# Joint image and text attention block: batch 0's image V first, batch 1's x loaded between V rows, text scores, gate and text V in one run of 32-column tiles

## The chip, the cores and the metric

The kernel runs on one core of a Trainium2 chip. The metric is the device time of one execution in microseconds. TensorE (PE) multiplies, VectorE (DVE), ScalarE (ACT) and GpSimd (POOL) work on tiles in SBUF and PSUM, and the queues of SyncE (SP), ACT and POOL issue the transfers (DMA).

## The reference

Two batches, 256 image tokens and 32 text tokens each, width D = 1152, bfloat16. With `c` the conditioning vector of a batch:

```
mod_i = (silu(c) @ wmod_img).reshape(B, 6, 1, D)      # rows 0, 1, 2: shift, scale, gate
mod_t = (silu(c) @ wmod_txt).reshape(B, 6, 1, D)
hi = layernorm(x_img) * (1 + sci) + shi ;  ht = layernorm(x_txt) * (1 + sct) + sht
qi, ki, vi = split(hi @ wqkv_img) ;        qt, kt, vt = split(ht @ wqkv_txt)
q, k, v = concat([qt, qi]), concat([kt, ki]), concat([vt, vi])      # 288 tokens
a = softmax(q k^T * D**-0.5) v
out_i = x_img + gai * (a[:, 32:] @ wo_img) ;  out_t = x_txt + gat * (a[:, :32] @ wo_txt)
```

## The kernel before, in words

D is nine slabs of 128 (`KT` = 9, `K8` = 8). Weight blocks of 1152 x 1152 come in one after the other on SP's queue, into five slots that are used again: image scale (`w_sc_i`), image V (`w_v_i`, in pieces of one, one, one, two, two and two slabs), image shift, image Q, and so on to the text output weights. The two batches of image x come first of all, one transfer each.

Image rows are four tiles of 128 (`NIT` = 4; tiles 0 and 1 are batch 0, tiles 2 and 3 batch 1). Each tile is normed: for tiles 0 and 2 ACT makes the sums (`ln_sums`), for 1 and 3 DVE the statistics (`ln_stats`); DVE norms all four (`ln_norm`). PE transposes the normed rows, three slabs of one batch at a time (`x_transposes`), into PSUM tiles `tp`; ACT or DVE copies these to `xT_i` (line 250).

The scale row of the modulation is made on PE with `silu(c)` as the stationary operand in four tiles of 32 columns (`sc_rows`, into `sc_ps`); DVE turns it into columns (`sc_cols`, line 257) and multiplies `xT_i` with it into `hS_i` (`x_scale`, line 264). V is made from `hS_i`, without the shift, which is added to attention's result later. `v_open` accumulates V over the slabs; six accumulators of 512 columns stand open at once: two for each of the tiles 0 and 1 (`A0`), one for each of the tiles 2 and 3 (`A1`). The two remaining ones follow, and `v_last` makes the last 128 columns of all four tiles. `evac` copies an accumulator to `v_i`, on DVE and ACT in turns. Between these parts stand the shift row (`mod_rows_of`, PSUM tile `gps`) and V's own shift (`shift_v_rows`).

Then come Q and K of the image (`qk_img`, 162 matmuls of 512 columns), with the text branch worked in between on DVE and ACT, then Q and K of the text.

The attention part: scores of image tiles (`scores_img`, nine matmuls for a tile), text scores in tiles of 32 columns (`scores_txt`), softmax in three steps (`soft_max` the row maximum on DVE, `soft_exp` the exponential on ACT, `soft_div` the division on DVE with 32 columns copied on POOL), transposes of the probabilities (`p_transposes`, PSUM tile `pT_ps`, ACT copies to `pT`), text V (`v_txt`, two halves `r`, in tiles of 64 columns that hold both batches' 32 tokens), the image gate (`mod_rows`: a row in four tiles of 32 columns, copied by ACT, written to DRAM by POOL's queue, and read back to all partitions as `gb` by `img_gate_spread`), `attn_pair` for weights times V, and the output projections `out_img` and `out_txt`.

PSUM has two pools: `ps_mm` with six places and `ps_tr` with two. A new tile waits until the one that had its place has been read. `pin` (`tc.keep_in_program_order`) keeps an instruction in the order of the program on its engine; all matmuls and transposes are pinned.

All matmuls are recorded at line 61 (`mm`) and all transposes at line 64 (`tr`), so the tile names tell them apart: `sc_ps`, `tp`, `vps` (V), `gps` (modulation rows), `ps` (Q, K, text V, output), `sps` (scores), `pT_ps`, `aps` (attention).

Of the kernel before, what the change touches and what calls it, by code (L numbers as in the profile page):

```python
# [14 lines left out]
def kernel(  # L15
# [14 lines left out]
    nc = tc.nc  # L30
# [32 lines left out]
    def tr(*a, **k):  # L63
        return pin(nc.tensor.transpose(*a, **k))  # L64
# [37 lines left out]
    sc_v, v_v = wview(wmod_img, D), wview(wqkv_img, 2 * D)  # L102
    for b in range(B):
        nc.sync.dma_start(x_i[:, b * TPB:(b + 1) * TPB, :], x_img[b].rearrange("(p t) d -> p t d", t=TPB))  # L104

# [3 lines left out]
    for r0, r1 in ((0, 1), (1, 2), (2, 3), (3, 5), (5, 7), (7, KT)):  # L109
        nc.sync.dma_start(w_v_i[:, r0:r1, :], v_v[:, r0:r1, :])  # L110
    w_sh_i = load_w(2, wmod_img, 0)
    w_q_i = load_rows(3, wqkv_img, 0)
    w_sh_t = load_rows(0, wmod_txt, 0, (0, 1, 3, 6))
# [99 lines left out]

    xn_i = act.tile([P, NIT, D], bf, tag="A")
    hS_i = act.tile([P, KT, B * NI], bf, tag="Bt")
# [11 lines left out]

    sc_ps = ps_mm.tile([P, KT, LW], f32, tag="mm")

# [10 lines left out]
    def x_transposes(k0, b):  # L240
        tr_pool = b == 1 or k0 < 6
        tp = (ps_tr if tr_pool else ps_mm).tile([P, 3, NI], bf, tag="tr" if tr_pool else "mm", name="tp")
        for kt in range(k0, k0 + 3):
            for t in range(TPB):
                i = b * TPB + t
                tr(tp[:, kt - k0, t * P:(t + 1) * P], xn_i[:, i, kt * P:(kt + 1) * P], ident[:])
# [19 lines left out]

    VW = 512
    v_i = act.tile([P, NIT, D], bf, tag="A")
    accs = {}

    def v_open(ids, k0, k1, kt_major=True):
        for key in ids:
            if key not in accs:
                accs[key] = ps_mm.tile([P, VW], f32, tag="mm", name="vps")
        loop = [(kt, key) for kt in range(k0, k1) for key in ids] if kt_major else \
            [(kt, key) for key in ids for kt in range(k0, k1)]
        for kt, (i, cc) in loop:
            mm(accs[(i, cc)][:], lhsT=hS_i[:, kt, i * P:(i + 1) * P], rhs=w_v_i[:, kt, cc * VW:(cc + 1) * VW],
               start=(kt == 0), stop=(kt == KT - 1), skip_group_check=True)
            if kt == KT - 1:  # L280
                evac(v_i[:, i, cc * VW:(cc + 1) * VW], accs[(i, cc)][:])

    A0 = [(0, 0), (0, 1), (1, 0), (1, 1)]
    A1 = [(2, 0), (3, 0)]

    def ln_norm_dve(i, mv):
        ln_norm(x_i[:, i, :], mv[:, 0:1], ln_rstd(mv[:, 1:2], P), P, xn_i[:, i, :])

    def ln_norm_act(i, sm):
        ln_norm(x_i[:, i, :], sm[:, 0:1], ln_rstd(sm[:, 2:3], P, sign=-1.0), P, xn_i[:, i, :])  # L290

    s0 = ln_sums(x_i[:, 0, :], xn_i[:, 0, :])
    m1 = ln_stats(x_i[:, 1, :], P, between=silu_cols)
    ln_var(s0)
    ln_norm_dve(1, m1)
    ln_norm_act(0, s0)
    s2 = ln_sums(x_i[:, 2, :], xn_i[:, 2, :])
    m3 = ln_stats(x_i[:, 3, :], P)
    ln_var(s2)
    r3, r2 = ln_rstd(m3[:, 1:2], P), ln_rstd(s2[:, 2:3], P, sign=-1.0)  # L300
    ln_norm(x_i[:, 3, :], m3[:, 0:1], r3, P, xn_i[:, 3, :])
    ln_norm(x_i[:, 2, :], s2[:, 0:1], r2, P, xn_i[:, 2, :])
    for out in [x_transposes(k0, 0) for k0 in (0, 3, 6)]:
        out()
    sc_rows(0, 4)
    warm_up(3)
    sc_rows(4, 7)
    out01 = x_transposes(0, 1)
    out31 = x_transposes(3, 1)
    sc_rows(7, K8)  # L310
    sc_rows(K8, KT)
    out61 = x_transposes(6, 1)
    out01()
    sc_cols(0, 1)
    x_scale(0, 1, 0, step=1)
    sc_cols(1, 5)
    x_scale(1, 3, 0)
    v_open(A0, 0, 3)
    out31()
    out61()  # L320
    x_scale(0, 3, 1)
    sc_cols(5, KT)
    for k0 in (3, 6):
        for b in range(B):
            x_scale(k0, k0 + 3, b)
    v_open(A1, 0, 3)
    v_open(A0 + A1, 3, KT - 2)
    v_open(A0 + A1, KT - 2, KT, kt_major=False)

# [7 lines left out]

    v_open([(2, 1)], 0, KT)
    p_sh = mod_rows_of(w_sh_i, sT32)
# [3 lines left out]
    for kt in range(KT):  # L343
        for b in range(B):
# [4 lines left out]
            else:  # L349
                nc.scalar.activation(h, h, ACT.Identity, bias=sh_i[:, kt, b:b + 1], scale=sc1_i[:, kt, b:b + 1])  # L350
    v_open([(3, 1)], 0, KT)

    def v_last():
        vps = ps_mm.tile([P, NIT, P], f32, tag="mm")
        for i in range(NIT):
            for kt in range(KT):
                mm(vps[:, i, :], lhsT=hS_i[:, kt, i * P:(i + 1) * P], rhs=w_v_i[:, kt, 2 * VW:D],
                   start=(kt == 0), stop=(kt == KT - 1))
        evac(v_i[:, :, 2 * VW:D], vps[:])

# [129 lines left out]
    def v_txt(r):  # L490
        ps = ps_mm.tile([P, VC], f32, tag="mm")
        for kt in range(KT):
            for g in range(2):
                c0 = g * HD + r * VC
                mm(ps[64 * g:64 * g + NTT, :], lhsT=hT_t[:, kt, :], rhs=w_v_t[:, kt, c0:c0 + VC],
                   start=(kt == 0), stop=(kt == KT - 1), tile_position=(0, 64 * g))
        return ps
# [10 lines left out]

    def mod_rows(w_blk, si):
        gps = ps_mm.tile([P, VC], f32, tag="mm")  # L510
        for kt in range(KT):
            for g in range(NGG):
                mm(gps[32 * g:32 * g + 32, :], lhsT=sT32[:, kt, :], rhs=w_blk[:, kt, g * VC:(g + 1) * VC],
                   start=(kt == 0), stop=(kt == KT - 1), tile_position=(0, 32 * g))
        g_sb = work.tile([P, VC], bf, tag="garow")
# [8 lines left out]
    def img_gate():  # L524
        mod_rows(w_ga_i, 0)

# [7 lines left out]
    def txt_gate():  # L534
        mod_rows(w_ga_t, 1)
        for g in range(2):
            for b in range(B):
                r0 = 64 * g + 32 * b
                nc.gpsimd.dma_start(gbf[r0:r0 + NT, :, :],
                                    gsc[1, b, :].rearrange("(r g j) -> g r j", r=2, g=2)[g].partition_broadcast(NT))  # L540

    v_last()
    shift_v_rows()
# [58 lines left out]

    def p_transposes(b):
        pT = work.tile([P, 3, NTOK], bf, tag="pT")
        tiles = [(range(3), ps_tr)] if b == 0 else [((2,), ps_mm), (range(2), ps_tr)]
        for kjs, pool in tiles:
            pT_ps = pool.tile([P, 8 * P], bf, tag="tr" if pool is ps_tr else "mm", name="pT_ps")
            txt = [(2, pbs["t"], ident2 if b else ident)]
            img = [(qi, pbs[(b, qi)], ident) for qi in range(TPB)]
            for n, kj in enumerate(kjs):  # L610
                for qi, pb, perm in (txt + img if b else img + txt):
                    o = n * NTOK + qpos[b][qi]
                    k0 = kj * P - (NT * b if kj == 2 else 0)
                    tr(pT_ps[:, o:o + P], pb[:, k0:k0 + P], perm[:])
            pin(nc.scalar.copy(pT[:, kjs[0]:kjs[-1] + 1, :],
                               pT_ps[:, 0:len(kjs) * NTOK].rearrange("p (k n) -> p k n", n=NTOK)))
        pTs[b] = pT

    def attn_keys(tiles, first):
        for b, dt in tiles:  # L620
            for kj in range(2):
                mm(tiles[(b, dt)][:], lhsT=v_i[:, b * TPB + kj, dt * P:(dt + 1) * P], rhs=pTs[b][:, kj, :],
                   start=(first and kj == 0), stop=(not first and kj == 1))
# [24 lines left out]

    sp = {key: scores_img(*key) for key in I[:2]}
    soft_max(I[0], sp[I[0]], P)  # L650
# [3 lines left out]
    soft_exp(I[1])  # L654
    st = scores_txt()
    half = work.tile([NTT, NTOK], f32, tag="half", bufs=1)
    pin(nc.scalar.copy(half[:], st[NTT:P, :]))
    soft_div(I[1])
    img_gate()
    pin(nc.vector.tensor_add(half[:], st[0:NTT, :], half[:]))  # L660
    soft_max("t", half, NTT)
    soft_exp("t")
    for key in I[2:]:
        sp[key] = scores_img(*key)
    soft_max(I[2], sp[I[2]], P)
# [86 lines left out]
```

## Time and profile before

| | us |
|---|---|
| median of 6 runs | 118.44 |
| lowest and highest | 117.76, 118.86 |
| the profiled execution | 118.42 |
| its span in the profile | 116.3 |

| engine | busy us | share of the span |
|---|---|---|
| PE (matmul) | 110.5 | 95% |
| DVE | 72.0 | 62% |
| PE (weight load) | 63.4 | 55% |
| ACT | 44.8 | 39% |
| POOL | 12.3 | 11% |

The profile is of one execution; its span runs from the first instruction of the program to the last, and some 2 us of the execution lie around it. "Chain" is the work that ended last, followed back step by step to what released it. An issue line names the transfer, its size and the time from issue to landing.

### The profile page before, as it was taken

The numbers are of one execution on the slowest core, as the hardware profiler recorded it, in microseconds if no ns is written. First come the engines' busy times: TensorE is split into PE (matmuls) and PEld (weight loads), VectorE is DVE, ScalarE is ACT, GpSimd is POOL, SyncE is SP. The second block draws the span as 40 slices with busy tenths as digits, with TensorE's granted clock in tenths as the row PEclk, the third lists the DMA queues.
The fourth block names the chain that finished last, engine by engine and source line by source line (L and its number), as shares of the span: only waits on it lengthen the run. The fifth ranks groups of instructions, "written<-read, shape, count | busy, mean of one in ns | idle before, by whom it ended". The sixth has DMA issues, their size and how long they took to land.

```text
span 116.3 us, 2500 instructions
## 1 busy us (share of the span) xinstructions
PE 110.5 (95%) x1036; PEld 63.4 (55%) x1036; DVE 72.0 (62%) x151; ACT 44.8 (39%) x93; POOL 12.3 (11%) x34
## 2 busy tenths in 40 slices
PE   5988899999999999999999999999999999999990
PEld 2335544445574444445454457777866555666670
DVE  3578494063869999999996040017748666356571
ACT  5699620042652298825241233245747400100000
POOL 7300000000000000000000000004618000443000
PEclk9999999999999999999999999999999999999999
DMA  3999999999999999999999999999999999722223
GB/s 103 386 384 408 406 407 410 414 410 412 409 401 411 332 409 413 403 414 411 409 358 411 414 410 418 399 419 399 411 401 412 422 385 403 280 110 56 101 51 102
DMA packets 18917, 41.02 MB, mean 353 GB/s; under 512 B 1323, under 2 KB 1851, under 8 KB 18907
## 3 DMA queue, kind: packets, MB, share of 16 engines
q1 hardware_dynamic: 18032, 39.85, 88.8%
q0 software_dynamic: 480, 0.89, 2.3%
q10 hardware_dynamic: 395, 0.12, 0.4%
q8 instruction: 8, 0.13, 0.4%
q14 instruction: 2, 0.02, 0.0%
HBM read 39.52 MB, written 1.34 MB: 351 GB/s over the span
## 4 chain that ended last, share of the span: by engine, by line
PE 85%; DMA 8%; DVE 2%; SPq 1%; ACT 1%; issue 0%
PE ps L61 52%; PE vps L61 15%; DMA t<-in_wmod_img_dram 8%; PE gps L61 5%; PE aps L61 5%; PE sps L61 5%; DVE tmp L693 1%; PE pT_ps L64 1%; PE tp L64 1%; DVE o L694 1%; SPq L104 1%; ACT xT_i L250 1%; PE sc_ps L61 0%; SPq L108 0%; PE tpt L64 0%
## 5 line engine op out<-in xcount | busy, mean ns | idle before, releaser
L61 PE MATMUL ps<-xT_i,t 128*128 128x512 bf16 x162 | 35.7, 379 | 0.0
L61 PEld LDWEIGHTS <-t 128*128 128x128 bf16 x324 | 20.5, 98 | 19.1 <-issue 0.6
L435 DVE SCALAR_TENSOR_TENSOR acc_sh<-t,sTf,acc_sh 128x1152 f32<-128x1152 bf16 x16 | 21.4, 1408 | 0.0
L61 PE MATMUL ps<-t,aT 128*128 128x384 bf16 (+3 forms) x153 | 20.3, 308 | 0.0
L61 PE MATMUL vps<-t,hS_i 128*128 128x512 bf16 (+1 forms) x108 | 17.9, 326 | 0.0
L61 PEld LDWEIGHTS <-aT 128*128 128x128 bf16 (+1 forms) x153 | 13.0, 101 | 7.1 <-issue 0.8
L61 PEld LDWEIGHTS <-hS_i 128*128 128x128 bf16 x108 | 9.0, 98 | 8.7 <-DVE hS_i L264 0.4
L365 ACT CAST qkT<-ps 128x512 bf16<-128x512 f32 (+2 forms) x11 | 6.1, 552 | 15.0 <-PE ps L61 13.7
L693 DVE TENSOR_TENSOR tmp<-ps,gb 128x384 bf16<-128x384 f32 (+2 forms) x13 | 6.8, 526 | 7.9 <-PE ps L61 7.9
L580 POOL TENSOR_SCALAR pb<-e,rs 128x32 bf16<-128x32 f32 (+1 forms) x5 | 2.1, 416 | 74.7 <-DVE rs L577 74.6
L363 ACT ACTIVATE qkT<-ps 128x512 bf16<-128x512 f32 (+2 forms) x11 | 6.1, 561 | 8.7 <-PE ps L61 7.0
L61 PE MATMUL wps<-warm 128*128 128x512 bf16 x25 | 7.6, 460 | 1.5 <-DVE unit L127 1.5
L180 DVE CAST v_i<-vps 128x512 bf16<-128x512 f32 x5 | 3.5, 692 | 7.5 <-PE vps L61 7.5
L565 DVE TENSOR_REDUCE nmx<-sps 128x1 f32<-128x288 f32 x4 | 1.8, 458 | 9.9 <-PE sps L61 9.9
L61 PEld LDWEIGHTS <-sT 128*32 128x32 bf16 x180 | 4.7, 96 | 2.9 <-issue 2.3
L182 ACT CAST v_i<-vps 128x512 bf16<-128x512 f32 x4 | 2.3, 580 | 9.9 <-PE vps L61 9.9
L629 DVE TENSOR_SCALAR aT<-aps,svc 128x288 bf16<-128x288 f32 x9 | 4.3, 518 | 2.1 <-PE aps L61 2.1
L61 PE MATMUL sps<-qkT 128*128 128x288 bf16 (+1 forms) x54 | 5.5, 287 | 0.0
L61 PE MATMUL ps<-hT_t,t 128*128 128x64 bf16 x162 | 5.2, 193 | 0.0
L61 PE MATMUL gps<-t,sT 128*32 128x288 bf16 x144 | 5.2, 287 | 0.0
L61 PEld LDWEIGHTS <-warm 128*128 128x128 bf16 x25 | 2.5, 111 | 4.9 <-issue 1.9
L61 PE MATMUL aps<-pT,v_i 128*128 128x288 bf16 x36 | 5.1, 287 | 0.0
(110 smaller groups left out, 105.1 us busy)
## 6 DMA issues: line engine op xcount, KB each, us to landing
t<-in_wqkv_txt_dram SPq DMA_DIRECT2D x3, 2592.0 KB, 18.5
t<-in_wmod_img_dram SPq DMA_DIRECT2D x2, 2592.0 KB, 14.0
t<-in_wmod_txt_dram SPq DMA_DIRECT2D x2, 2592.0 KB, 18.7
t<-in_wqkv_img_dram SPq DMA_DIRECT2D x3, 864.0 KB, 13.8
t<-in_wqkv_img_dram SPq DMA_DIRECT2D x1, 2592.0 KB
t<-in_wo_img_dram SPq DMA_DIRECT2D x3, 864.0 KB, 9.2
t<-in_wqkv_img_dram SPq DMA_DIRECT2D x3, 576.0 KB, 10.0
t<-in_wmod_txt_dram SPq DMA_DIRECT2D x2, 864.0 KB, 12.8
```

The lines of the kernel that those rows point to most:

```text
L61: return pin(nc.tensor.matmul(*a, **k))
L64: return pin(nc.tensor.transpose(*a, **k))
L104: nc.sync.dma_start(x_i[:, b * TPB:(b + 1) * TPB, :], x_img[b].rearrange("(p t) d -> p t d", t=TPB))
L180: nc.vector.tensor_copy(out_ap, in_ap)
L182: nc.scalar.copy(out_ap, in_ap)
L363: nc.scalar.mul(out_ap, in_ap, SCALE)
L365: nc.scalar.copy(out_ap, in_ap)
L435: pin(nc.vector.scalar_tensor_tensor(acc, w_sh_t[:, kt, :], col, acc, op0=ALU.mult, op1=ALU.add))
L565: pin(nc.vector.reduce_max(nmx[0:qn, :], sps[0:qn, :], axis=AX.X, negate=True))
L580: pin(nc.gpsimd.tensor_scalar(pb[0:qn, NI + 2 * NT:NI + 3 * NT], e[0:qn, NI:NTOK], rs[0:qn, :], 0.0, op0=ALU.mult, op1=ALU.add))
L629: nc.vector.tensor_scalar(dst, tiles[(b, dt)][:], bias, None, op0=ALU.add)
L693: nc.vector.tensor_mul(tmp[:, 0:n], ps[:, 0:n], gb[:, b, c0:c0 + n])
```

## The change

At the start, only batch 0's x is loaded ahead of the scale weights. The two tiles of batch 1 come as two transfers of 288 KB, one behind V's second piece and one behind V's fourth. `w_q_i` is loaded in two pieces instead of three. The normed rows and V are kept in one tile for each batch (`xn_b`, `v_b`).

Batch 0 is normed, transposed and scaled in all nine slabs before batch 1's norms begin. V has accumulators of 384 columns: batch 0's six run over slabs 0 to 7; then come 12 transposes of batch 1, slab 8 for four accumulators, the other 6 transposes, slab 8 for the last two; batch 1's accumulators follow, two together and then one by one. `v_last` is gone. The evacuations of batch 0's V are assigned to ACT or DVE by a string. The PSUM places of `sc_ps` and of batch 0's `tp` change pools, and two warm-up matmuls stand between the scale rows instead of three.

In the attention part PE makes the scores of all four image tiles, then text scores, the image gate's rows and text V in one run. Text V is made in tiles of 32 columns, one for each half of the columns and each batch. The softmax steps follow in a new order; the gate row's copy and writes (`gate_row`) stand behind the division of the text rows. The probabilities of batch 0 are transposed in two parts (slabs 0 and 1, and slab 2), and slab 2's copies of both batches are made by DVE instead of ACT.

```diff
-    for b in range(B):
-        nc.sync.dma_start(x_i[:, b * TPB:(b + 1) * TPB, :], x_img[b].rearrange("(p t) d -> p t d", t=TPB))
+    nc.sync.dma_start(x_i[:, 0:TPB, :], x_img[0].rearrange("(p t) d -> p t d", t=TPB))
...
     for r0, r1 in ((0, 1), (1, 2), (2, 3), (3, 5), (5, 7), (7, KT)):
         nc.sync.dma_start(w_v_i[:, r0:r1, :], v_v[:, r0:r1, :])
+        if r0 in (1, 3):
+            i = TPB + r0 // 2
+            nc.sync.dma_start(x_i[:, i, :], x_img[1].rearrange("(p t) d -> t p d", t=TPB)[i - TPB])
     w_sh_i = load_w(2, wmod_img, 0)
-    w_q_i = load_rows(3, wqkv_img, 0)
+    w_q_i = load_rows(3, wqkv_img, 0, (0, 5))
...
-    sc_ps = ps_mm.tile([P, KT, LW], f32, tag="mm")
+    sc_ps = ps_tr.tile([P, KT, LW], f32, tag="tr")
...
-        tr_pool = b == 1 or k0 < 6
-        tp = (ps_tr if tr_pool else ps_mm).tile([P, 3, NI], bf, tag="tr" if tr_pool else "mm", name="tp")
+        tp = (ps_tr if b else ps_mm).tile([P, 3, NI], bf, tag="tr" if b else "mm", name="tp")
...
+    V0, V1 = [[(i, cc) for i in range(b * TPB, (b + 1) * TPB) for cc in range(NCH)] for b in range(B)]
...
-    s2 = ln_sums(x_i[:, 2, :], xn_i[:, 2, :])
-    m3 = ln_stats(x_i[:, 3, :], P)
-    ln_var(s2)
-    r3, r2 = ln_rstd(m3[:, 1:2], P), ln_rstd(s2[:, 2:3], P, sign=-1.0)
-    ln_norm(x_i[:, 3, :], m3[:, 0:1], r3, P, xn_i[:, 3, :])
-    ln_norm(x_i[:, 2, :], s2[:, 0:1], r2, P, xn_i[:, 2, :])
     for out in [x_transposes(k0, 0) for k0 in (0, 3, 6)]:
         out()
     sc_rows(0, 4)
-    warm_up(3)
     sc_rows(4, 7)
-    out01 = x_transposes(0, 1)
-    out31 = x_transposes(3, 1)
+    warm_up(1)
     sc_rows(7, K8)
+    warm_up(1)
     sc_rows(K8, KT)
-    out61 = x_transposes(6, 1)
-    out01()
     sc_cols(0, 1)
     x_scale(0, 1, 0, step=1)
     sc_cols(1, 5)
-    x_scale(1, 3, 0)
-    v_open(A0, 0, 3)
+    x_scale(1, 4, 0)
+    sc_cols(5, KT)
+    x_scale(4, KT, 0)
+    s2 = ln_sums(x_i[:, 2, :], xn_b[1][:, 0, :])
+    ln_var(s2)
+    m3 = ln_stats(x_i[:, 3, :], P)
+    r2, r3 = ln_rstd(s2[:, 2:3], P, sign=-1.0), ln_rstd(m3[:, 1:2], P)
+    ln_norm(x_i[:, 2, :], s2[:, 0:1], r2, P, xn_b[1][:, 0, :])
+    ln_norm(x_i[:, 3, :], m3[:, 0:1], r3, P, xn_b[1][:, 1, :])
+    v_open(V0, 0, K8)
+    out01, out31 = x_transposes(0, 1), x_transposes(3, 1)
+    out01()
     out31()
-    out61()
-    x_scale(0, 3, 1)
-    sc_cols(5, KT)
-    for k0 in (3, 6):
-        for b in range(B):
-            x_scale(k0, k0 + 3, b)
-    v_open(A1, 0, 3)
-    v_open(A0 + A1, 3, KT - 2)
-    v_open(A0 + A1, KT - 2, KT, kt_major=False)
+    x_scale(0, 6, 1)
+    v_open(V0[0:4], K8, KT, engines="AAVV")
+    x_transposes(6, 1)()
+    v_open(V0[4:], K8, KT, engines="AA")
+    x_scale(6, KT, 1)
+    v_open(V1[0:2], 0, KT)
...
-    v_open([(2, 1)], 0, KT)
+    v_open(V1[2:3], 0, KT)
...
-    v_open([(3, 1)], 0, KT)
...
+    for key in V1[3:]:
+        v_open([key], 0, KT)
...
-                c0 = g * HD + r * VC
-                mm(ps[64 * g:64 * g + NTT, :], lhsT=hT_t[:, kt, :], rhs=w_v_t[:, kt, c0:c0 + VC],
-                   start=(kt == 0), stop=(kt == KT - 1), tile_position=(0, 64 * g))
+                for b in range(B):
+                    c0, r0 = g * HD + r * VC, 64 * g + NT * b
+                    mm(ps[r0:r0 + NT, :], lhsT=hT_t[:, kt, NT * b:NT * b + NT], rhs=w_v_t[:, kt, c0:c0 + VC],
+                       start=(kt == 0), stop=(kt == KT - 1), tile_position=(0, r0))
...
-    v_last()
     shift_v_rows()
...
-    sp = {key: scores_img(*key) for key in I[:2]}
+    sp = {key: scores_img(*key) for key in I}
+    st = scores_txt()
+    img_gate()
+    vt = [v_txt(0)]
+    half = work.tile([NTT, NTOK], f32, tag="half", bufs=1)
     soft_max(I[0], sp[I[0]], P)
     soft_exp(I[0])
     soft_max(I[1], sp[I[1]], P)
     soft_div(I[0])
     soft_exp(I[1])
-    st = scores_txt()
-    half = work.tile([NTT, NTOK], f32, tag="half", bufs=1)
+    soft_max(I[2], sp[I[2]], P)
+    soft_div(I[1])
+    soft_exp(I[2])
+    soft_max(I[3], sp[I[3]], P)
+    soft_div(I[2])
     pin(nc.scalar.copy(half[:], st[NTT:P, :]))
-    soft_div(I[1])
-    img_gate()
+    soft_exp(I[3])
     pin(nc.vector.tensor_add(half[:], st[0:NTT, :], half[:]))
     soft_max("t", half, NTT)
+    soft_div(I[3])
     soft_exp("t")
-    for key in I[2:]:
-        sp[key] = scores_img(*key)
-    soft_max(I[2], sp[I[2]], P)
-    soft_exp(I[2])
     soft_div("t")
-    soft_max(I[3], sp[I[3]], P)
-    soft_exp(I[3])
-    soft_div(I[2])
-    soft_div(I[3])
-    p_transposes(0)
-    for r in range(2):
-        v_txt_out(r, v_txt(r))
-    p_transposes(1)
+    gate_row()
+    v_txt_out(0, vt[0])
+    vt.append(v_txt(1))
+    p_transposes(0, (0, 1), ps_tr, nc.scalar.copy)
+    v_txt_out(1, vt[1])
+    p_transposes(0, (2,), ps_mm, nc.vector.tensor_copy)
+    p_transposes(1, (2,), ps_mm, nc.vector.tensor_copy)
+    p_transposes(1, (0, 1), ps_tr, nc.scalar.copy)
     img_gate_spread()
```

More of the change, by code (lines that the diff above doesn't have):

```diff
@@ L212, in ln_norm @@
         pin(nc.vector.tensor_scalar(out_ap, x_ap, mean, rstd[0:np_, :], op0=ALU.subtract, op1=ALU.mult))
-    xn_i = act.tile([P, NIT, D], bf, tag="A")
+    xn_b = [act.tile([P, TPB, D], bf, tag="A%d" % b, name="xn%d" % b) for b in range(B)]
     hS_i = act.tile([P, KT, B * NI], bf, tag="Bt")
@@ L240, in x_transposes @@
     def x_transposes(k0, b):
-        tr_pool = b == 1 or k0 < 6
-        tp = (ps_tr if tr_pool else ps_mm).tile([P, 3, NI], bf, tag="tr" if tr_pool else "mm", name="tp")
+        tp = (ps_tr if b else ps_mm).tile([P, 3, NI], bf, tag="tr" if b else "mm", name="tp")
         for kt in range(k0, k0 + 3):
             for t in range(TPB):
-                i = b * TPB + t
-                tr(tp[:, kt - k0, t * P:(t + 1) * P], xn_i[:, i, kt * P:(kt + 1) * P], ident[:])
+                tr(tp[:, kt - k0, t * P:(t + 1) * P], xn_b[b][:, t, kt * P:(kt + 1) * P], ident[:])
         dst = xT_i[:, k0:k0 + 3, b * NI:(b + 1) * NI]
@@ L265, in x_scale, with v_open @@
                                             op0=ALU.mult))
-    VW = 512
-    v_i = act.tile([P, NIT, D], bf, tag="A")
+    v_b = [act.tile([P, TPB, D], bf, tag="A%d" % b, name="v%d" % b) for b in range(B)]
     accs = {}
-    def v_open(ids, k0, k1, kt_major=True):
+    def v_open(ids, k0, k1, engines=None):
         for key in ids:
             if key not in accs:
[L274 to L278, printed above, removed]
+                accs[key] = ps_mm.tile([P, CH], f32, tag="mm", name="vps")
+        for kt, (i, cc) in [(kt, key) for kt in range(k0, k1) for key in ids]:
+            mm(accs[(i, cc)][:], lhsT=hS_i[:, kt, i * P:(i + 1) * P], rhs=w_v_i[:, kt, cc * CH:(cc + 1) * CH],
                start=(kt == 0), stop=(kt == KT - 1), skip_group_check=True)
             if kt == KT - 1:
-                evac(v_i[:, i, cc * VW:(cc + 1) * VW], accs[(i, cc)][:])
-    A0 = [(0, 0), (0, 1), (1, 0), (1, 1)]
-    A1 = [(2, 0), (3, 0)]
+                dst = v_b[i // TPB][:, i % TPB, cc * CH:(cc + 1) * CH]
+                if engines:
+                    pin((nc.scalar.copy if engines[ids.index((i, cc))] == "A" else nc.vector.tensor_copy)(
+                        dst, accs[(i, cc)][:]))
+                else:
+                    evac(dst, accs[(i, cc)][:])
+    V0, V1 = [[(i, cc) for i in range(b * TPB, (b + 1) * TPB) for cc in range(NCH)] for b in range(B)]
     def ln_norm_dve(i, mv):
-        ln_norm(x_i[:, i, :], mv[:, 0:1], ln_rstd(mv[:, 1:2], P), P, xn_i[:, i, :])
+        ln_norm(x_i[:, i, :], mv[:, 0:1], ln_rstd(mv[:, 1:2], P), P, xn_b[i // TPB][:, i % TPB, :])
     def ln_norm_act(i, sm):
-        ln_norm(x_i[:, i, :], sm[:, 0:1], ln_rstd(sm[:, 2:3], P, sign=-1.0), P, xn_i[:, i, :])
-    s0 = ln_sums(x_i[:, 0, :], xn_i[:, 0, :])
+        ln_norm(x_i[:, i, :], sm[:, 0:1], ln_rstd(sm[:, 2:3], P, sign=-1.0), P, xn_b[i // TPB][:, i % TPB, :])
+    s0 = ln_sums(x_i[:, 0, :], xn_b[0][:, 0, :])
     m1 = ln_stats(x_i[:, 1, :], P, between=silu_cols)
@@ L350 @@
                 nc.scalar.activation(h, h, ACT.Identity, bias=sh_i[:, kt, b:b + 1], scale=sc1_i[:, kt, b:b + 1])
-    v_open([(3, 1)], 0, KT)
[L353 to L359, printed above, removed]
+    for key in V1[3:]:
+        v_open([key], 0, KT)
     def qk_evac(out_ap, in_ap, blk):
@@ L507, in v_txt_cols, with mod_rows @@
         return r0, v_t[r0:r0 + NT, c0:c0 + P]
-    def mod_rows(w_blk, si):
+    def mod_rows(w_blk):
         gps = ps_mm.tile([P, VC], f32, tag="mm")
@@ L514, in mod_rows, with mod_row_out @@
                    start=(kt == 0), stop=(kt == KT - 1), tile_position=(0, 32 * g))
+        return gps
+    def mod_row_out(gps, si):
         g_sb = work.tile([P, VC], bf, tag="garow")
@@ L524, in img_gate, with gate_row @@
     def img_gate():
-        mod_rows(w_ga_i, 0)
+        rows["gi"] = mod_rows(w_ga_i)
+    def gate_row():
+        mod_row_out(rows["gi"], 0)
     def img_gate_spread():
@@ L534, in txt_gate @@
     def txt_gate():
-        mod_rows(w_ga_t, 1)
+        mod_row_out(mod_rows(w_ga_t), 1)
         for g in range(2):
@@ L601, with p_transposes @@
     pTs = {}
[L603 to L617, printed above, removed]
+    def p_transposes(b, kjs, pool, copy):
+        pT_ps = pool.tile([P, 8 * P], bf, tag="tr" if pool is ps_tr else "mm", name="pT_ps")
+        txt = [(2, pbs["t"], ident2 if b else ident)]
+        img = [(qi, pbs[(b, qi)], ident) for qi in range(TPB)]
+        for n, kj in enumerate(kjs):
+            for qi, pb, perm in (txt + img if b else img + txt):
+                o = n * NTOK + qpos[b][qi]
+                k0 = kj * P - (NT * b if kj == 2 else 0)
+                tr(pT_ps[:, o:o + P], pb[:, k0:k0 + P], perm[:])
+        if b not in pTs:
+            pTs[b] = work.tile([P, 3, NTOK], bf, tag="pT", name="pT")
+        pin(copy(pTs[b][:, kjs[0]:kjs[-1] + 1, :],
+                 pT_ps[:, 0:len(kjs) * NTOK].rearrange("p (k n) -> p k n", n=NTOK)))
     def attn_keys(tiles, first):
@@ L621, in attn_keys @@
             for kj in range(2):
-                mm(tiles[(b, dt)][:], lhsT=v_i[:, b * TPB + kj, dt * P:(dt + 1) * P], rhs=pTs[b][:, kj, :],
+                mm(tiles[(b, dt)][:], lhsT=v_b[b][:, kj, dt * P:(dt + 1) * P], rhs=pTs[b][:, kj, :],
                    start=(first and kj == 0), stop=(not first and kj == 1))
```

## The prediction

> **What bounds the kernel now.** I read the page first: one engine fills the span.
>
> ```profile
> PE 110.5 (95%) x1036; PEld 63.4 (55%) x1036; DVE 72.0 (62%) x151; ACT 44.8 (39%) x93; POOL 12.3 (11%) x34
> GB/s 103 386 384 408 406 407 410 414 410 412 409 401 411 332 409 413 403 414 411 409 358 411 414 410 418 399 419 399 411 401 412 422 385 403 280 110 56 101 51 102
> PE 85%; DMA 8%; DVE 2%; SPq 1%; ACT 1%; issue 0%
> ```
>
> Matmul work holds 85% of the chain that ended last, and the transfers run at some 410 GB/s through the first hundred microseconds. So a change counts by when PE starts, how long its instructions are, and where it is made to wait. Next the chain of waits in order of time (start, length, what), at the two places that the diff touches.
>
> ```profile
> 2.12 9.78 DMA t<-in_wmod_img_dram
> ...
> 14.34 13.77 PE vps L61 x63
> 28.11 1.22 PE gps L61 x36
> 29.33 4.06 PE vps L61 x45
> 33.39 1.22 PE gps L61 x36
> 34.60 19.53 PE ps L61 x90
> ...
> 76.28 2.93 PE sps L61 x36
> 79.21 1.10 PE gps L61 x36
> 80.31 2.31 PE sps L61 x18
> 82.62 0.50 PE pT_ps L64 x9
> 83.12 2.33 PE ps L61 x36
> 85.45 0.61 PE pT_ps L64 x9
> 86.06 5.78 PE aps L61 x54
> 91.83 5.85 PE ps L61 x36
> ```
>
> Before 14.34 the chain is a transfer, the scale weights. From 14.34 on PE runs without a hole in either place. Any microsecond in which PE starts earlier is won only if PE then keeps running; any wait put into these two stretches is paid in full. Last, the timeline and the transfers, for the start of V and the arrival of one piece of its weights.
>
> ```profile
> 9.79 0.38 SPq L110 DMA_DIRECT2D t<-in_wqkv_img_dram  x1
> 13.20 0.45 PE L61 MATMUL sc_ps<-t,sT 128*32 128x288 bf16 x8
> 14.03 0.42 DVE L264 TENSOR_SCALAR hS_i<-xT_i,scc 128x128 bf16<-128x128 bf16 x2
> ```
>
> ```profile
> t<-in_wqkv_img_dram SPq DMA_DIRECT2D x1, 576.0 KB, 9.0
> ```
>
> The last scale rows come at 13.3 and V starts 1.03 later. The transfer issued at 9.79 is V rows 5 and 6; it lands 9.0 later, at 18.8.
>
> **First stretch, start.** The 576 KB of batch 1's x now stand behind V rows. At the 408 GB/s of that slice this is 1.44 us, and all four pieces of scale weights land that much earlier: the last at 11.9 instead of 13.3, V starts at 12.93. Nothing else holds it: batch 0's transposes end at 9.78 in the trace, and their three copies (ACT 0.80 twice, DVE 0.55) no longer stand behind batch 1's sums and norms, so they end near 10.8. Fewer warm-up matmuls (2 for 3) cost nothing: they lay in PE's idle time; the granted clock reads 9 in every slice, and the holes left are below 1 us. SP makes 16 issues up to w_q as before (one x issue more, one w_q issue less); an issue takes about 0.4 us, and the weights queued on the DMA engines cover that.
>
> **First stretch, work.** V goes from 72 matmuls of 512 columns and 36 of 128 (13.77 + 4.06 = 17.83 us in the chain) to 108 of 384. The output projection has that shape: 36 in 5.85, 0.1625 each, so 17.55. The 18 transposes of batch 1 lay before V and now stand inside it: 0.0556 each by the 9 in 0.50 on the chain, 0.064 by the 12 between 12.43 and 13.20; I take 1.05 for all (ends 1.0 and, by the 6 in 0.51 from 13.83 to 14.34, which hold a wait, 1.5). The two gps blocks stay at 2.44. Without waits the projection of Q would start at 12.93 + 17.55 + 1.05 + 2.44 = 33.97, 0.63 before the 34.60 of now.
>
> **First stretch, waits.** Batch 0's six accumulators take 6 x 0.1625 = 0.975 for each of V's rows of weights, and a row of 288 KB takes 0.72 to arrive, but x of batch 1 now stands between the rows. V rows 0 and 1 land at 12.6 and 13.35 and row 2, behind one x piece, at 14.8: in time. Rows 3 and 4 land at 16.2, PE is ready at 15.86. Rows 5 and 6 have the same bytes ahead of them as before, so I put them at 18.8 again; PE would be ready at 16.2 + 1.95 = 18.15 and, never held up, at 17.81. So 1.0 us of the earlier start is given back here. Bounds: 18.35 by the spacing of the neighbours (16.91 + 1.44), 19.2 if the lag that grew by 0.4 between these two pieces grows as much again. From 18.81 on: rows 5 to 7, 18 x 0.1625 = 2.93, to 21.74.
>
> The Trainium skill speaks against this order: in "DMA: Bandwidth & Descriptors", Specifications, it puts a limit of about 358 GB/s on what HBM gives one core; at that rate 576 KB would take 1.65 us, the start would gain more and rows 5 and 6 would come later. The slices above read 408 to 414 during V, so the measured rate decides.
>
> Then come 12 transposes of batch 1 (0.7), row 8 for four accumulators (0.65), 6 transposes (0.35) and row 8 for two (0.33), to 23.8. Norms are ready: x piece 2 lands near 14.1 and ACT's sums (1.16 + 1.16 + 2 x 0.19) end at 16.7; piece 3 lands at 16.9, three statistics of 0.55, the aggregate, two rstd steps and two norms of 0.58 end at 19.9, under PE's rows 5 to 7. If that cover went, the 12 transposes would slip by as much. Now two new waits. First, batch 1's first accumulators need the places of batch 0's: ACT has the copy of transposes (0.80) ahead of the two evacuations (0.5 each), which end near 23.5 and 24.0 against 23.8 and 23.95 on PE: 0.1. Second, DVE's order is a copy (0.55, from 22.5), six scalings (0.277 each), two evacuations, and only then the scalings of rows 6 to 8. An evacuation of 384 columns lies between 0.458 (288 columns, subtraction) and 0.692 (512); I take 0.55 as for the 384-column multiply. Row 6 is scaled at 23.0 + 1.66 + 1.1 + 0.28 = 26.05, and PE wants it at 25.8: 0.3. Together 0.4, ends 0 and 0.8; queued behind it is the whole of V's batch 1.
>
> Sum from 18.81: 2.93 + 1.05 + 6 x 0.1625 + 54 x 0.1625 + 2.44 = 16.17, to 34.98, with 0.4 of waits to 35.4. Against 34.60 that is 0.8 later. Shift and scale of hT (DVE 12 x 0.26, ACT 6 x 0.5, from 30.5) end near 34 beside V, as before. w_q is complete by 33.1 in the trace, so it isn't late either. Until the scores PE is back to back and all slides by this amount; DVE's shift chain has 4.4 us of slack (its wait for shps).
>
> **Second stretch.** Now: 2.93 + 1.10 + 2.31 + 0.50 + 2.33 + 0.61 = 9.78 from the scores to attention. 18 image score matmuls alone are 2.20; the 2.31 holds 0.11 of going back from tiles to the full array, and the 2.33 another 0.13 over 18 pairs at 0.122. After: 2 x 2.20 + 0.73 (text scores, with the way into tiles) + 1.10 (gate) + 2 x 1.10 (text V, now 72 instructions of 32 columns at the gate's rate) + 0.50 + 0.61 = 9.54, a gain of 0.24. Ends: the gate's other two blocks took 1.22, so text V could cost 2.44 and the gain is 0; if each step between modes costs 0.25, it is 0.5.
>
> The Trainium skill speaks against the narrower instructions: "TensorEngine Tiling (Array Packing)", Instruction Overhead, puts about 60 cycles on each matmul. As an estimate at the 2.4 GHz that the page "TensorE: Matmul & The Clock Gate" names, 36 more of them would be 0.9 us, and the stretch would lose 0.7 instead of gaining 0.24. The gate's block of 36 such instructions in 1.10 (0.031 each, four side by side) shows no such cost in this trace, so the row decides.
>
> What this order can lose: softmax of the third and fourth image tile no longer has text V behind it alone. ACT: half copy (0.40, from 81.25), fourth exponential to 82.25, text exponential to 83.3 (behind DVE's add and maximum, 0.45 each), gate copy 0.40. DVE: text division to 83.9, text V out to 84.6 and 85.05. PE ends text V at 84.45, transposes to 85.6; ACT's copy (0.64, from 85.0) ends at 85.65. Attention starts at 85.7 on this clock, with a wait of 0.05. Upper end 0.5, a quarter microsecond for each of ACT's two copies. The gate row's two writes (POOL, 0.63 each) now stand behind the text division, issued near 84 instead of 81.06; landing 4.4, then gb 5.7: gb is there near 95, and the first multiply wants it at 93.3. DVE needs 0.92 for a chunk and PE 1.46, with six banks, so DVE catches up and PE doesn't see it; uncovered it would be 1.7. Text weights w_v_t land at 80.0, needed at 82.3. Image evacuations in attention swap engines (518 against 499 ns): nothing. Taken: 0.2 gained.
>
> **Sum.** 0.8 - 0.2 = 0.6 on the profiled run's 118.42 us (span 116.3, 2.1 around it; the median of the runs is 118.44): 119.1 with rounding up for the small waits of semaphores that I left out.
>
> **Rivals.** (1) V's supply keeps up. If rows 5 and 6 land by 17.81, PE never starves in V and only the 0.4 of other waits is left: 33.97 + 0.4 = 34.4, and with the 0.2 the kernel takes 118.0; with those waits gone too, 117.6. It decides from a landing at 18.2, where the sum is zero. For it: lags between 1.4 and 1.9 us from last packet to landing, so the 18.81 may be bad luck. Against: the bytes ahead are the same. Half way (18.35 and half the waits) is no change, 118.4. (2) The second stretch turns into a wait of 0.5 or more: ACT's chain from half to the copies of pT is late and attention starts after 86.2; 119.8. For it: a margin of 0.05. Against: every duration in it is from a row. (3) Batch 1's transposes wait for the norms or the places: another 0.5 to 0.8, 119.9.
>
> **Chances.** Forecast case (118.8 to 119.6) 0.47; rival 1 in full 0.15, half way 0.2; rivals 2 and 3 together 0.18. About 0.5%, 0.6 us, is what a measurement of this kernel can tell from no change. Slower by more than that: two thirds of the forecast case and rivals 2 and 3, 0.5. Faster by more: 0.16. Within: 0.34. The range 117.8 to 119.9 leaves out the end of rival 1 and the tails of 2 and 3.
>
> **What would show it.** Right: first V matmul near 12.9; holes on PE near 16 and 18.5 put down to w_v's transfer; a hole near 26 put down to hS_i; Q's first matmul near 35.4; scores to attention 9.5 to 9.6. Wrong: V without holes, Q before 34.6, or a hole before aps put down to ACT's pT.

## The result and the profile after

The changed kernel takes 119.0 us against 118.18 us before (medians of 22 and 46 runs); the ratio is 1.0069 with a 95% interval of 1.0052 to 1.0086. That is 0.8 us slower, where 0.7 had been forecast. Medians are of all executions; the ratios, here and below, leave out those that took over 1.5% longer than the fastest of the same kernel. The profiled execution took 119.05 us with a span of 117.1, against 118.42 and 116.3.

The page after, engines and shares of the chain:

```profile
PE 110.4 (94%) x1071; PEld 64.8 (55%) x1071; DVE 71.3 (61%) x153; ACT 45.6 (39%) x95; POOL 12.4 (11%) x34
PE 79%; DMA 14%; DVE 2%; SPq 1%; ACT 1%; issue 0%
```

PE does as much as before, but 14% of the chain is now a transfer, and six points less are PE. The chain in order of time (start, length, what) says where:

```profile
2.19 8.31 DMA t<-in_wmod_img_dram
10.50 0.02 issue
10.52 8.53 DMA t<-in_wqkv_img_dram
19.04 0.04 issue
19.08 3.09 PE vps L61 x18
22.17 0.67 PE tp L64 x12
22.84 0.65 PE vps L61 x4
23.49 0.40 PE tp L64 x6
23.89 4.71 PE vps L61 x29
28.60 1.22 PE gps L61 x36
29.82 4.49 PE vps L61 x27
34.31 1.22 PE gps L61 x36
35.52 19.53 PE ps L61 x90
...
77.10 5.13 PE sps L61 x54
82.23 1.10 PE gps L61 x36
83.33 2.21 PE ps L61 x72
85.54 0.46 PE pT_ps L64 x6
85.99 0.02 issue
86.01 0.65 ACT pT L612
86.66 0.04 issue
86.70 5.94 PE aps L61 x54
92.64 5.85 PE ps L61 x36
```

V's first 30 matmuls are not on it at all: the chain goes from V's weight rows 5 and 6, issued at 10.52 and landed at 19.04, to the matmuls that use them. In the second stretch ACT's copy of `pT` has come in between the transposes and attention. PE's timeline shows V's start and the hole:

```profile
12.61 5.13 PE L61 MATMUL vps<-t,hS_i 128*128 128x384 bf16 x30 [0.69 <-DVE hS_i L264]
19.08 0.32 PE L61 MATMUL vps<-t,hS_i 128*128 128x384 bf16 x1 [1.34 <-DMA t<-in_wqkv_img_dram]
```

From PE's timelines, the first matmul of each stage:

| | V | Q | scores | attention | output |
|---|---|---|---|---|---|
| before | 14.34 | 34.53 | 76.12 | 85.89 | 91.67 |
| changed | 12.61 | 35.46 | 76.94 | 86.70 | 92.48 |
| difference | -1.73 | +0.93 | +0.82 | +0.81 | +0.81 |

V starts 1.73 us earlier and from V to Q it takes 22.85 instead of 20.19. From the first score to attention nothing is gained: 9.76 against 9.77. Between Q and the scores 0.11 is made up; nothing here shows why.

One more line of both pages, which the prediction didn't use: each has eight transfers of the kind "instruction", blocks of an engine's program. One of them falls in V. What moved from 16.6 to 17.7 us in the changed kernel, by queue:

```profile
q1 hardware_dynamic: 200, 0.43, 99.4%
q8 instruction: 1, 0.02, 5.5%
```

It is a packet of 16 KB that lasts from 16.67 to 17.64; a weight packet of 2.3 KB takes 0.09 on its DMA engine. The kernel before has the same packet at 15.89 to 16.82.

The trace also holds sixteen completion marks for each of these weight transfers, as many as the core has DMA engines. Of the marks of rows 5 and 6 fifteen come from 17.21 to 17.77 and one at 19.04. For the piece before them (x's last) all sixteen come from 15.78 to 16.35; for rows 7 and 8 again one is late, at 20.43 against 19.19. So one engine's share of the bytes holds up the whole piece, as it would if the packet of 16 KB stood in front of that share.

### The profile page after: what moved, and what is told of

It is laid out like the page before. It is cut to its first block, busy times and chain, and to the rows that moved or that the text cites. A ratio compares the mean times of both kernels' runs of the same rounds, so it can differ in the third digit from the quotient of the medians.

```text
span 117.1 us, 2573 instructions
## 1 busy us (share of the span) xinstructions
PE 110.4 (94%) x1071; PEld 64.8 (55%) x1071; DVE 71.3 (61%) x153; ACT 45.6 (39%) x95; POOL 12.4 (11%) x34
## 4 chain that ended last, share of the span: by engine, by line
PE 79%; DMA 14%; DVE 2%; SPq 1%; ACT 1%; issue 0%
PE ps L61 52%; PE vps L61 11%; DMA t<-in_wqkv_img_dram 7%; DMA t<-in_wmod_img_dram 7%; PE gps L61 5%; PE aps L61 5%; PE sps L61 4%; DVE tmp L692 1%; PE tp L64 1%; SPq L107 1%; DVE o L693 1%; ACT pT L612 1%; PE pT_ps L64 0%; SPq L103 0%; PE tpt L64 0%
## 5 line engine op out<-in xcount | busy, mean ns | idle before, releaser
L61 PEld LDWEIGHTS <-t 128*128 128x128 bf16 x324 | 20.5, 98 | 18.9 <-issue 0.5
L61 PE MATMUL vps<-t,hS_i 128*128 128x384 bf16 x108 | 18.5, 327 | 2.0 <-DMA t<-in_wqkv_img_dram 1.3
L61 PEld LDWEIGHTS <-hS_i 128*128 128x128 bf16 x108 | 10.3, 98 | 9.2 <-issue 1.8
L250 ACT COPY xT_i<-tp 128x768 bf16<-128x768 bf16 x4 | 3.1, 808 | 5.2 <-PE tp L64 5.2
L61 PE MATMUL aps<-pT,v 128*128 128x288 bf16 x36 | 5.1, 287 | 0.1
L627 ACT ACTIVATE aT<-aps,svc 128x288 bf16<-128x288 f32 x9 | 4.3, 501 | 1.6 <-PE aps L61 1.6
## 6 DMA issues: line engine op xcount, KB each, us to landing
t<-in_wqkv_txt_dram SPq DMA_DIRECT2D x3, 2592.0 KB, 17.7
t<-in_wqkv_img_dram SPq DMA_DIRECT2D x1, 1440.0 KB, 17.7
```

Source lines behind the costliest of these rows:

```text
L61: return pin(nc.tensor.matmul(*a, **k))
L627: nc.scalar.activation(dst, tiles[(b, dt)][:], ACT.Identity, bias=bias)
```

## The experiments

Ratios are against runs of the kernel before on the same chip.

**Each half alone.** e1 has the new first stretch and the old second; e2 the old first and the new second. The edits are the two halves of the change's diff.

> The new first stretch (x and V order) with the old second stretch (scores to attention). Theory 1, the first stretch alone loses: Q starts near 35.5 as in the changed kernel, attention 9.77 after the first score as before, 0.8 to 0.9 us slower than before. Theory 2, both stretches take part, the second one losing what its wait before attention costs: 0.5 to 0.6 us slower than before here, the rest in the other half.

> The old first stretch with the new second stretch (one run of 32-column tiles). Theory 1: the tiled run saves 0.2 and the wait for ACT's copy of pT gives it back, so scores to attention stay at 9.75 and the time is that of before within 0.1 us. Theory 2: slower than before by 0.2 to 0.3 us. By the term on record (0.2 gained, 0.05 waited) it would be 0.2 us faster.

e1: 118.85 us, ratio 1.0024 (0.9998 to 1.0050). Q at 35.62, rows 5 and 6 again late (PE goes on with row 5 at 19.25), first score to attention 9.78. e2: 118.56 us, ratio 0.999 (0.9959 to 1.0020); Q at 34.59, first score to attention 9.76. Its chain has the same piece of ACT:

```profile
84.76 0.46 PE pT_ps L64 x6
85.21 0.02 issue
85.23 0.65 ACT pT L621
85.88 0.04 issue
85.92 5.94 PE aps L61 x54
```

By its stages the new second stretch costs nothing and gains nothing, as theory 1 has it; the 0.2 us that the prediction gave it are missing. (The times alone can't say so: 0.2 us lies inside e2's interval.) e1's stages are those of theory 1, its time is less above before than either theory has it (0.3 us, at most 0.6), and less than the whole change's. The halves' intervals together just reach the whole; the times can't divide the loss more finely than that, and the profiles put all of it ahead of Q.

**Is the supply of V rows the loss?** e4 takes batch 1's x away from among V's rows; batch 1 is normed from batch 0's x. (This kernel leaves out batch 1's own norms.)

```diff
-        if r0 in (1, 3):
-            i = TPB + r0 // 2
-            nc.sync.dma_start(x_i[:, i, :], ...)
+    nc.sync.dma_start(x_i[:, TPB:NIT, :], ...)       # behind all of w_v_i
-    s2 = ln_sums(x_i[:, 2, :], xn_b[1][:, 0, :])
+    s2 = ln_sums(x_i[:, 0, :], xn_b[1][:, 0, :])     # m3 and both norms likewise
```

> The changed kernel with batch 1's x loaded behind all of V; batch 1 is normed from batch 0's x, so its result is left out, and the work of every engine is the same. Supply theory: rows 5 and 6 land 1.4 earlier, at 17.6 to 17.8, as PE wants them; the hole of 1.3 goes, Q near 34.0, 1.3 to 1.5 us faster than the changed kernel. Rival, dependencies of the new order: the hole stays, within 0.3 us of the changed kernel.

117.73 us, ratio 0.9914 (0.9883 to 0.9944). Q at 34.01. Its chain runs through V's first eight rows in one piece:

```profile
12.75 7.97 PE vps L61 x48
```

Rows 5 and 6 land at 16.7 there. V to Q takes 21.26 where the changed kernel takes 22.85: late weights cost 1.6 us in all. The rest of the new order (copies, places, scalings) leaves 0.2 over the 21.04 of plain work.

**x ahead, as it was.** e3 loads batch 1's x ahead of the scale weights again and keeps everything else.

> The changed kernel with batch 1's x loaded ahead of the scale weights again, all else new. Supply theory: V starts near 14.0, rows 5 and 6 land where they did (near 19.0) and PE is ready for them only then, so the hole goes but the start is lost: Q near 35.2, 0.2 to 0.4 us faster than the changed kernel. Rival, the waits come from the new order of transposes, copies and scalings: the hole of 1.3 stays beside the late start, Q near 36.5, 1 us slower than the changed kernel.

120.15 us, ratio 1.0099 (1.0063 to 1.0135). The hole before row 5 is gone, but this run answers another question: with two warm-up matmuls and later scale rows, PE was busy for only 0.75 of the 2 us from 10 to 12, and the granted clock fell afterwards. The view by windows (PE busy, granted clock in the column after POOL):

```profile
12.00:14.50 2.50, 1.74 (x22) 0.72 (x21) 0.26 (x2) 1.15 (x2) 0.00 (x0) 1.00 1.04 401
14.50:17.90 3.40, 3.13 (x10) 1.49 (x11) 3.36 (x15) 0.50 (x2) 0.00 (x0) 0.50 1.04 411
```

The clock is at 0.50 for 3.4 us, and V begins in that stretch, at 14.77. This is one execution, with a mean clock of 0.986; the seven of the twelve in which it was 0.996 or more took 119.2 to 120.3 us. So e3b adds `warm_up(5)` between the first two groups of scale rows:

> As e3 (batch 1's x ahead of the scale weights, else the changed kernel), with five more warm-up matmuls between the first and second group of scale rows, so that PE isn't idle there. In e3 the granted clock was 0.5 from 14.5 to 17.9 us. Supply theory: with the clock at 1.0 V starts near 14.2, no hole behind it, Q near 35.2: 0.2 to 0.4 us faster than the changed kernel. Rival (waits of the new order): Q near 36.5, 1 us slower than the changed kernel. If the clock falls again the idle time wasn't its cause.

119.22 us, ratio 1.0111 (1.0077 to 1.0146). The clock stays at 1.0, V starts at 14.47, no hole follows, V to Q takes 21.27, Q is at 35.74. The rival is out: the new order has no large waits of its own (0.2 over the plain work, as in e4). But it isn't faster than the changed kernel either, as I had expected; the start came 0.3 later than I had put it. Moving x and putting transposes inside V must be told apart: with the supply complete, the new order needs 21.27 against 20.19, because 18 transposes that PE did while it waited for the scale weights now stand inside V. That is 1.08, close to the 1.05 of the prediction; small waits and V's better shape nearly cancel. Loading batch 1's x later then buys 1.9 at the start of V (12.61 against 14.47) and pays 1.6 in late weights.

**Why are rows 5 and 6 so late?** In the changed kernel each piece up to x's last one lands about 0.6 after its last byte has moved, rows 5 and 6 land 1.8 after it. (Moved means here that the queue's bytes, counted over all engines, have passed the end of the piece.) The 16 KB packet lies just there. In e4, where the pieces are others, rows 5 and 6 are through before it (its packet lies at 16.51 to 17.44) and land in time, and rows 7 and 8 come 2.5 after them (19.16) instead of 1.4; fifteen of their marks are there by 18.11. e5 was to move the packet by making PE's warm-up of fewer, longer instructions:

```diff
-    warm_up(8)
+    warm_up(4)
+    warm_long(2)          # f32, 256 columns
...
-    warm_up(14)
+    warm_long(7)
```

> The changed kernel with eighteen warm-up instructions of PE fewer: nine f32 matmuls of 256 columns stand for eighteen bf16 ones of 512, so PE's instruction load of 16 KB (16.67 to 17.64 in the changed kernel) is asked for nine matmuls later. Theory, that load delays rows 5 and 6 by about 1 us on the DMA engine it uses: rows 5 and 6 land near 17.8, the hole of 1.3 shrinks to 0.2, Q near 34.4, 1 us faster than the changed kernel. Rival, the bytes ahead alone set the landing: rows 5 and 6 at 19.0 again, no change beyond 0.2 us.

118.94 us, ratio 1.0074 (1.0042 to 1.0107). Inconclusive: the nine f32 matmuls were carried out as 18 matmuls and 18 weight loads, so PE's count did not change; the packet (16.52) and the landing (18.90) moved by only 0.15. e10 takes instructions away instead:

```diff
-    warm_up(14)
+    warm_up(5)
```

> The changed kernel with 5 warm-up matmuls instead of 14 ahead of the first transposes, 18 instructions of PE fewer (in e5 the nine f32 matmuls were run as eighteen, so PE's count had not changed). Theory, PE's 16 KB instruction load makes rows 5 and 6 late: the load starts later than 17.8, rows 5 and 6 land near 17.9 instead of 19.04, the hole before row 5 goes from 1.3 to 0.2, Q near 34.4. Rival, the bytes ahead and not the load: rows 5 and 6 land at 19.0 again. If the granted clock falls for want of warm-up, V starts later than 12.9 and the time says nothing; the landing still does.

118.74 us, ratio 1.0004 (0.9982 to 1.0025). The packet moves to 17.94, PE goes on with row 5 at 18.07 instead of 19.08, and the wait appears two rows later. Its timeline, and the queues from 17.9 to 18.9:

```profile
16.68 3.50 PE L61 MATMUL vps<-t,hS_i 128*128 128x384 bf16 x19
20.55 1.14 PE L61 MATMUL vps<-t,hS_i 128*128 128x384 bf16 x6 [0.38 <-DMA t<-in_wqkv_img_dram]
```

```profile
q1 hardware_dynamic: 180, 0.38, 98.8%
q8 instruction: 1, 0.02, 5.8%
```

The theory holds: the bytes ahead of rows 5 and 6 are the same, the packet has moved, and they land at 18.02 with no mark left behind. Rows 7 and 8 have fifteen marks by 19.46 and the last at 20.51. So the packet belongs to PE's code, and what is in flight when it is loaded lands about a microsecond late, whichever rows it is. Q is at 34.98, not 34.4: by the starts of its matmuls PE waits 0.54 before row 7, and 0.26 before each of the rows 3 and 5. The mean clock was 0.998 in the profiled execution.

**Smaller pieces.** e7 loads V rows 3 to 6 one by one, at the same bytes and order.

```diff
-    for r0, r1 in ((0, 1), (1, 2), (2, 3), (3, 5), (5, 7), (7, KT)):
+    for r0, r1 in ((0, 1), (1, 2), (2, 3), (3, 4), (4, 5), (5, 6), (6, 7), (7, KT)):
...
-        if r0 in (1, 3):
-            i = TPB + r0 // 2
+        if r0 in (1, 4):
+            i = TPB + r0 // 4
```

> The changed kernel with V rows 3 to 6 loaded one by one instead of in pairs; the bytes, their order and the x pieces between them are the same. Supply theory: row 5 can be used when its own 288 KB are there, 0.7 earlier than the pair: PE's hole before row 5 goes from 1.3 to 0.6 or, where row 5's packets pass before the instruction load, to 0.2; row 6 then comes at 19.0 against 18.9. 0.5 to 1.1 us faster than the changed kernel. Rival, the pair's size plays no part: no change.

118.73 us, ratio 1.0055 (1.0026 to 1.0085). Row 5 (issued at 11.55) and row 6 (12.22), from the transfers:

```profile
t<-in_wqkv_img_dram SPq DMA_DIRECT2D x1, 288.0 KB, 5.8
t<-in_wqkv_img_dram SPq DMA_DIRECT2D x1, 288.0 KB, 6.6
```

Row 5 lands at 17.3 with all its marks, row 6 at 18.8 with one mark 0.8 behind the rest (the packet lies at 16.37 to 17.25). By the starts of the matmuls holes of 0.3 (before row 6) and 0.4 (before row 7) are left, and Q is at 34.68, 0.78 earlier than in the changed kernel. By the ratios the gain over the changed kernel is 0.2 us, and the two intervals overlap; by the other kernels of the same chip (e5, e6) it is 0.2 to 0.4, less than the 0.5 to 1.1 expected. Part of the 0.78 is lost at the end: from the start of PE's last matmul to the end of the span it takes 3.71 us in e7, and 3.7 in e11 and e13, which also load V's rows one by one, against 3.35 in the changed kernel and the one before. What takes these 0.36 us isn't shown.

**The copy of pT.** e6 splits the copy of batch 0's two slabs, one to ACT and one to DVE.

```diff
-    p_transposes(0, (0, 1), ps_tr, nc.scalar.copy)
+    p_transposes(0, (0, 1), ps_tr, (nc.scalar.copy, nc.vector.tensor_copy))   # one slab each
```

> The changed kernel with the copy of batch 0's first two slabs of pT split: slab 0 on ACT, slab 1 on DVE. Theory, attention waits 0.2 for ACT's copy of 0.65: first score to attention 9.55 instead of 9.76, 0.2 us faster than the changed kernel. Rival, attention is held by text V on DVE or by the transposes themselves: no change.

119.1 us, ratio 1.0104 (1.0075 to 1.0133). First score to attention is 9.55, as expected, and more than that gain is lost at once: attention takes 6.17 instead of 5.78. On DVE the second slab waits for ACT's half, and text V's second half waits behind it:

```profile
86.04 0.40 ACT L614 COPY pT<-pT_ps 128x288 bf16<-128x288 bf16 x1 [1.38 <-PE pT_ps L64]
...
86.47 0.31 DVE L614 COPY pT<-pT_ps 128x288 bf16<-128x288 bf16 x1 [0.91 <-ACT pT L614]
...
86.81 0.46 DVE L493 TENSOR_TENSOR v_t<-ps,svb 128x288 bf16<-128x288 f32 x1
```

e11 and e12 change the engines about instead: text V's second half first on DVE, then the two-slab copies on DVE, the one-slab copies on ACT.

```diff
-    p_transposes(0, (0, 1), ps_tr, nc.scalar.copy)
     v_txt_out(1, vt[1])
-    p_transposes(0, (2,), ps_mm, nc.vector.tensor_copy)
-    p_transposes(1, (2,), ps_mm, nc.vector.tensor_copy)
-    p_transposes(1, (0, 1), ps_tr, nc.scalar.copy)
+    p_transposes(0, (0, 1), ps_tr, nc.vector.tensor_copy)
+    p_transposes(0, (2,), ps_mm, nc.scalar.copy)
+    p_transposes(1, (2,), ps_mm, nc.scalar.copy)
+    p_transposes(1, (0, 1), ps_tr, nc.vector.tensor_copy)
```

> e7 (V rows 3 to 6 loaded one by one) with the four copies of pT changed about: the two-slab copies on DVE behind text V's second half, the one-slab copies on ACT. Theory, attention waits for ACT's copy of 0.65 and DVE does it in 0.42 while ACT's two take 0.40 each: first score to attention 9.57 instead of 9.77, attention itself 5.8 as in the changed kernel, 0.2 us faster than e7. Rival, the wait moves into attention as it did in e6 (6.17): no faster than e7.

> e2 (the first stretch of before, the new second stretch) with the copies of pT changed about as in e11. Theory: Q at 34.5 to 34.6, first score to attention 9.57, attention 5.8: 0.2 us faster than before and the fastest of all here. Rival: the gain goes into attention, same as before within 0.1 us.

e11: 118.31 us, ratio 0.9971 (0.9958 to 0.9984). e12: 118.54 us, ratio 0.9987 (0.9972 to 1.0002). Both take 9.59 from the first score to attention and 5.77 to 5.78 for attention; the 0.2 is there. e11's timeline:

```profile
85.09 0.46 DVE L493 TENSOR_TENSOR v_t<-ps,svb 128x288 bf16<-128x288 f32 x1
85.52 0.46 DVE L612 COPY pT<-pT_ps 128x576 bf16<-128x576 bf16 x1
...
86.03 0.90 PE L61 MATMUL aps<-pT,v 128*128 128x288 bf16 x6
```

DVE copies two slabs in 0.46 where ACT takes 0.65, and attention starts as the last transpose is through. e11 (single V rows and this) is faster than both kernels. In e11's profiled execution V starts at 13.34 and Q at 34.99, later than in the profile of before; the gain is in the times, not in the early stages of this profile. e12's gain of 0.15 us is near the expected size, but its interval takes in no change, and its Q is at 34.91 instead of 34.5 to 34.6 (V starts at 14.72).

**All of it.** e13 is e11 with every V row by itself and 5 warm-up matmuls.

> The changed kernel with all three mended: every V row loaded by itself, 5 warm-up matmuls instead of 14 (the instruction load near 18), the copies of pT as in e11. Theory: rows 5, 6 and 7 are there when PE wants them, no hole in V above 0.2, Q 21.3 after V (near 34.0), first score to attention 9.58; 1.2 us faster than e10 and 0.9% faster than before. Rival, supply is late anyway after the instruction load: a hole of 0.5 before row 7 or 8, 0.5% faster than before.

118.81 us, ratio 0.9974 (0.9931 to 1.0016): not shown to be faster. V starts at 12.58, Q is at 34.38, a hole of 0.55 before row 7 is left by the starts of the matmuls, as the rival has it; row 7's last mark is 1.5 behind the other fifteen. Eleven of its twelve executions fall in two groups: at a mean granted clock of 0.996 or more, five took 117.4 to 117.9 us; at 0.985, six took 118.7 to 119.0. The twelfth, at 0.966, took 120.1. Four of e10's twelve show the 0.985 too, while none of the 42 executions of the changed kernel, e7 and e11, with 14 warm-up matmuls, is under 0.994. So the warm-up that was taken away to shift the code load had been holding the clock.

## Why the prediction was right, point by point

- **Sign and place held; the reason held in part, and the size by luck.** Q was to start at 35.4 and started at 35.46; the loss was to sit in V, on the transfer of rows 5 and 6, and e4 shows that it does. That the bytes ahead make them late is a small part of it (see Supply). Three of the terms behind that sum were mis-sized (the start by 0.3, the supply by 0.6, the other waits by 0.4), and they cancelled.
- **The signs**: V's start (to 0.3), the hole on w_v's transfer before row 5 and Q came as listed. The hole near 16 was only 0.1, the one near 26 didn't come, scores to attention took 9.76 instead of 9.5 to 9.6, and one sign of being wrong did appear: the wait before `aps` put down to ACT's `pT`.
- **Start of V**: 12.93 predicted, 12.61 measured. The scale weights' pieces came sooner than by the 1.44 of x's bytes: in the changed kernel pieces land some 0.6 after their last byte has moved, in the one before 1.3. In the kernel before one of the sixteen marks trails the rest by 0.85 to 0.99 from the first piece of the scale weights (9.77) to rows 3 and 4 (16.91); in the changed kernel none trails by more than 0.14 until the packet. What held that engine back wasn't found.
- **Work in V**: 21.04 without waits; 21.26 and 21.27 in e4 and e3b. Held to 0.2.
- **Supply**: 1.0 predicted, 1.6 measured by e4. This is the term that was most off. I put rows 5 and 6 at 18.8 because the bytes ahead of them stay the same, and allowed that the lag which the trace of before shows there was bad luck. It goes with PE's code load, which is in that trace too, on the page's list of queues: fourteen of the marks of rows 5 and 6 are there by 17.44, and two are late, at 18.40 and 18.81, where the pieces ahead had one late mark. PE came to those rows later there and did not wait. In the changed kernel the bytes ahead alone would have had rows 5 and 6 there at 17.77 by their fifteenth mark, some 0.2 after PE wanted them; the code load put 1.27 on top. So the 18.8 was near for a reason that the prediction didn't have, and its rival 1 was right that the bytes let them land earlier.
- **Places and evacuations**: 0.4 predicted, none measured. After its 12 and 6 transposes PE ran 29 matmuls in 4.71 without a wait; the 0.2 that e4 has over the plain work isn't put down to any of these. DVE's six scalings took 1.26, not 1.66, and its two evacuations 1.01, not 1.1, so row 6 was scaled in time. Six in a row took 0.21 each, not the 0.277 that was taken for one.
- **Second stretch**: a gain of 0.2 predicted, none measured. The work shrank as said: 5.13 + 1.10 + 2.21 on the chain, against 5.13 + 1.10 + 2.20 in the sum. The wait for ACT's copy was put at 0.05 and is 0.2; e11 and e12 show that without it the 0.2 is gained. The error is one of reading: the chain's 86.06 for before is the modelled end of the last transpose, while attention's first matmul started 0.17 earlier, at 85.89. The 0.05 was counted from such a modelled end; without a wait PE would have started before it.
- **gb** came late, as said: DVE waited 3.9 us for it, more than the 1.7 of the sum, and PE did not see it.
- **The rivals**: the supply that keeps up (rival 1) is what e4 makes by force. Rival 2 took place in small, at 0.2, with the mechanism it names. Rival 3 did not occur; the transposes found their norms done at 19.3.

## What to carry to other kernels

In this kernel, loading later what is needed later would only have paid if PE hadn't caught up with the rows that now stood behind it: count arrivals and demand row by row, and count the work that used to fill the old wait as lost cover. A wait is for a whole piece, so a piece of weights that is as small as the step that consumes it shortens the wait; here that gained 0.2 to 0.4 us of the time (e7). When a wait is moved off PE, look which engine's queue the freed work lands in; a gain of 0.2 us was lost to ACT's copy in the changed kernel, and to the order of work on DVE in e6. When a figure is carried over from a trace, ask what is in it: the landing at 18.8 had a code load in it, and what moves the code moves that landing.

## What the runs showed of the hardware that was not expected

- PE's code comes in packets of 16 KB over the same DMA engines, eight in the span; one lasted 0.97 us, and one of the sixteen completion marks of the pieces in flight came 1.0 to 1.3 us after the other fifteen (changed kernel, e4, e10). Taking 18 PE instructions away moved the packet by 1.27 us and the late mark with it (e10). The Trainium skill, "Runtime: NRT & Kernel Launch", Instruction fetch mechanics, has the blocks of 16 KiB (256 instructions) and a DMA queue for them, and calls the cost of crossing one mostly hidden; in this kernel PE isn't seen waiting for the code itself, but it waits for the weights that the code held up: 1.27 of the 1.5 us before row 5 lie between the fifteenth mark and the last.
- With PE busy for 2.49 of the 4.5 us from 10.0 to 14.5, the granted clock went to 0.50 for 3.4 us (e3); with five more warm-up matmuls there (busy 3.34 of 4.5) the mean was 0.998 or more in all six executions (e3b), where e3 had five of twelve at 0.986 or less.
- V's start goes with the time at which the granted clock first rises to 1.0: 5.97 us in the changed kernel's profile, 7.42 and 7.45 in e1's and e11's, whose V starts at 13.3 instead of 12.6. Warm-up matmuls start 0.43 apart before that time and 0.22 after it, so that from 6.0 to 7.4 us PE ran 8 of them in the first and 5 in the others.
- A call of an f32 matmul with 256 columns ran as two matmuls, recorded at 0.44 us each, and two weight loads (e5).
